# An earlier load of the second block's query features, four averages in one run, and the last keys' sums ahead of a turning, in a two-layer linear-attention and Mish kernel

## The chip, the core and the metric

The kernel runs on one core of a Trainium2 chip. The time is the device time of one execution in microseconds (us); the median of several runs counts. Before the change it is 1363.09 us (three runs, 1362.66 to 1363.34).

## What is computed

The input x has 2048 tokens (rows) of 640 numbers. Two layers are applied one after the other, each made of an attention part A and a dense part B, both with a layer norm ahead and a residual:

```python
x = x + A(layernorm(x)); x = x + B(layernorm(x))    # twice, same weights
# A: 32 heads of 20
pq = q @ w_phi;  pk = k @ w_phi                      # per head
phi_q = concat(softmax(pq), softmax(-pq));  phi_k = the same of pk      # 40 per head
kv = phi_k^T v  (summed over all tokens);  z = phi_k summed over all tokens
o = (phi_q kv) / (phi_q z + 1e-6);  out = o @ wo
# B: h = x w1 + b1;  act = h * tanh(softplus(h));  out = act @ w2       # 1536 hidden
```

No token's output o can be had before kv and z are complete, that is before the keys of the last token are summed.

## The kernel before

The 2048 tokens are 16 tiles of 128 (numbered 0 to 15), two tiles to a block (eight blocks, 0 to 7). In what follows K14 is the work on the keys of tile 14, Q14 on its queries, V14 on its values. TensorE is PE, VectorE DVE, ScalarE ACT, GpSimd POOL; all DMAs are issued from SyncE's queue, SP. A full-precision product is made of three matmuls of a high and a low part of each operand (line 399), and "splitting" is the making of these parts: a copy on ACT and a subtraction on another engine.

**First stage** (`attend_first`, line 448). For each block in turn the keys, values and queries of its two tiles are projected on PE (`project`, lines 387 to 400). `features` (lines 415 to 441) makes the softmax features out of a projection: ACT copies them out of PSUM, DVE takes maximum and minimum (429), POOL or DVE subtracts (430, 432), ACT takes the exponential, DVE sums and inverts (438, 439), POOL multiplies (440). Key features are then multiplied with the values and summed into one PSUM bank, `kva`, that stays open through the stage (line 475, 64 matmuls to a tile; two tiles follow one another directly). Query features are turned by a DVE transpose (484) and stored to DRAM with four DMAs (488), into `e_d[b]`.

These steps are Python generators. `advance` (461) resumes every pending generator once, the youngest first, after each new projection; so the yields say how far apart in the program the steps of one tile lie. The order of the last block is K14, K15, V14, V15, Q14 (line 649); Q15 is left to the second stage.

**Second stage** (`attend_second`, line 733). `finish_kv` (716) copies `kva`, turns it and masks it into `kvb`. `load(b)` (705) brings the turned query features of a block back: two tiles of five groups (712) and a small one (713). `average(b, t)` (743) multiplies them with `kvb` (753, 44 matmuls) into a PSUM tile of two banks and divides on DVE (762 to 767). `Transposed.step` turns the quotients of a block on PE (311) and splits them (127 on ACT, 317 on DVE). `Rows.half` (780) projects them with wo (399) and adds the residual. Between them the first stage's last projection Q15 is made and its features are finished bit by bit (`rest`, 687). In this order the stage starts: half of Q15, the sums of K14 and K15, `kva`'s copy, load(1), more of Q15, average(0,0), average(0,1), load(2), average(1,0), the turning of block 0, average(1,1), load(3), and then the loop over the blocks.

**Dense part** (`dense`, line 845), eight blocks of six pairs of hidden tiles. While the last pair runs, `load_v_weights` (185) loads and splits the value weights of the next layer (`split`, 134; `V_ORDER` is 0, 1, 4, 2, 3). Each of the five goes through a staging tile: two row tiles, two `v` tiles, one `big` tile.

**Buffers that the change touches.** `big` tiles (five): key features, every third tile's query features, loaded query features, the dense part's scratch. `x` tiles (two): the residual rows of a block. `r2` wide tiles 10 and 11: query features of the other tiles (`query_tile`, 412), later weights of the dense part. `v` tiles (two): value rows, and the turned inputs of the next block. PSUM: two `mm` tiles of two banks, four `one` tiles of one bank, of which `kva` holds one during the first stage.

**Order.** Everything lies in a block whose order is planned per engine on a simulated timeline when the kernel is built. In the second stage PE and SP keep the written order; DVE, ACT and POOL are planned everywhere in the lines that the change touches. An engine takes its instructions in that fixed order and waits where an operand isn't there.

Of the kernel before, what the change touches and what calls it, by code (L numbers as in the profile page):

```python
# [8 lines left out]
F32 = mybir.dt.float32  # L9
# [12 lines left out]
DH = 20  # L22
KD = D // P
KF = F // P
BT = 2
# [26 lines left out]
def kernel(  # L52
# [22 lines left out]
    def mm_tile():  # L75
        return psum.tile([P, 2, 512], F32, tag="mm", name="mm", bufs=2)
# [4 lines left out]
    def big_tile():  # L81
        return work.tile([P, EW], F32, tag="big", name="big", bufs=5)
# [4 lines left out]
    def pair_tile(dtype=F32R):  # L87
        return work.tile([P, 2, BLK], dtype, tag="ol", name="ol", bufs=6)
# [80 lines left out]
    def r2_wide(j, dtype=F32R):  # L169
        return wts.tile([P, 2, D], dtype, tag=f"r2{j}", name=f"r2{j}")  # L170
# [4 lines left out]
            return w[:, 0], w[:, 1]  # L175
        return tuple(wts.tile([P, D], F32R, tag=f"r2{s}{j}", name=f"r2{s}{j}") for s in "hl")

    def v_weights(ws, low=nc.vector):

        for k in V_ORDER:  # L180
            split(ws[k][0][:, D:2 * D], ws[k][1][:, D:2 * D], wv[k * P:(k + 1) * P, :],
                  (row_tile, row_tile, v_tile, v_tile, big_tile)[k], low)
            yield

    def load_v_weights():

        ws = [r1_pair(k) for k in range(KD)]
        for _ in v_weights(ws):
            pass
        return ws  # L190

# [218 lines left out]
        return g % 4, 2 * DH * (3 * (g // 4) + j)  # L410

    def query_tile(i):
        return big_tile() if i % 3 == 2 else r2_wide(10 + i % 3, F32).rearrange("p s d -> p (s d)")

    def features(ps, e, pool_sub):

# [31 lines left out]
    def attend_first(layer, x_src, first):  # L448
# [31 lines left out]
        def queries(xts, i, ps=None):  # L480
            e = query_tile(i)
            yield from features(project(xts, i % BT, q_ws, 0, w=FC) if ps is None else ps, e, True)

            nc.vector.transpose(e, e)  # L484
            b, t = divmod(i, BT)
            dst = e_d[b].rearrange("(j f) (t q s) -> t q f j s", f=32, t=BT, s=32)
            for q in range(4):
                nc.sync.dma_start(dst[t, q], e[32 * q:32 * q + 32].rearrange("f (j s) -> f j s", s=32))
                if b == NB - 1:
                    yield  # L490
# [150 lines left out]
        for b in range(0 if layer else 1, NB):  # L641
            xts = nxt
            order = ("k0", "k1", "v0", "v1", "q0", "q1")
            if b == 0:
                order = ("v0", "k0", "k1", "v1", "q0", "q1")
            elif b == 1 and layer == 0:
                order = ("k0", "q0", "k1", "v0", "q1", "v1")
            elif b == NB - 1:
                order = ("k0", "k1", "v0", "v1", "q0")
            vs = [v_tile() for _ in range(BT)]  # L650
            for n, (kind, t) in enumerate(order):
                t = int(t)
                i = b * BT + t
                if b == 0 and n == 1:
                    kva = one_tile()
                    nc.vector.memset(kva[:, :360], 0.0)
                if b == NB - 1 and n == 3:
                    loaded = {0: load(0)}
                if b + 1 < NB:
                    if n == 0 and b == 1 and layer == 0:  # L660
                        with tc.issue_after(ready):
                            xt = fetch_normed(b + 1)
                    elif n == 0:
                        xt = fetch_normed(b + 1)
# [37 lines left out]

        return kva, o_ws, loaded, rest()

    def load(b):

        ta, tb, tc_ = big_tile(), big_tile(), pair_tile(F32)
        for t, g0 in ((ta, 0), (tb, 5)):

            src = e_d[b][120 * g0:120 * (g0 + 4) + P]  # L710
            src = bass.AP(tensor=src.tensor, offset=src.offset, ap=[[BLK, P], [120 * BLK, 5], [1, BLK]])
            nc.sync.dma_start(t.rearrange("f (g s) -> f g s", s=BLK), src)
        nc.sync.dma_start(tc_[:80, 0], e_d[b][1200:])
        return [(ta, tb)[g // 5][:, (g % 5) * BLK:(g % 5 + 1) * BLK] for g in range(10)] + [tc_[:, 0]]
# [18 lines left out]
    def attend_second(x_src, x_dst, acc, fetches, makes, fetch_next, begin_next):  # L733
# [6 lines left out]
            with tc.issue_after(div[0]):  # L740
                next(rest, None)

        def average(b, t):

            phs = loaded[b]
            po = mm_tile()
            for g in range(G):
                n = 120 if g < 10 else 80
                w = GW if g < 10 else 42
                c, j = divmod(g, 8)  # L750
                for q in range(2):
                    s0 = t * P + 64 * q
                    nc.tensor.matmul(  # L753
                        po[64 * q:64 * q + 64, c, GW * j:GW * j + w], phs[g][:n, s0:s0 + 64],
                        kvb[:n, g, :w], start=True, stop=True)
            o = row_tile()
            den = work.tile([P, H], F32, tag="r", name="den", bufs=2)
            pv = [po[:, c, :(DH + 1) * n].rearrange("p (h d) -> p h d", d=DH + 1)
                  for c, n in ((0, 24), (1, 8))]
            hh = (slice(0, 24), slice(24, H))  # L760
            for c in range(2):
                nc.vector.tensor_scalar_add(den[:, hh[c]], pv[c][:, :, DH], DEN_EPS)
            nc.vector.reciprocal(den, den)
            for c in range(2):
                n = hh[c].stop - hh[c].start
                ins = nc.vector.tensor_tensor(o.rearrange("p (h d) -> p h d", d=DH)[:, hh[c]], pv[c][:, :, :DH],
                                        den[:, hh[c]].unsqueeze(2).to_broadcast([P, n, DH]), op=ALU.mult)
                div[0] = ins.ins
            rows.setdefault(b, []).append(o)
            if t == BT - 1:  # L770
                del loaded[b]

        class Rows:

# [16 lines left out]
        with tc.manual_schedule(engines={mybir.EngineType.PE, mybir.EngineType.SP}):  # L791
            kv = finish_kv(kva)
            next(rest)
            next(kv)
            loaded[1] = load(1)
            xs = {0: fetch(x_src, 0)}
            fetches[0]()
            next(rest)
            next(kv)
            next(rest)  # L800
            average(0, 0)
            average(0, 1)
            loaded[2] = load(2)
            average(1, 0)
            cur = Transposed(rows.pop(0)).all()
            average(1, 1)
            loaded[3] = load(3)
            for b in range(NB):
                if b == NB - 1:
                    ahead.all()  # L810
                elif b:
                    average(b + 1, 0)
                    average(b + 1, 1)
                r0, r1 = Rows(b, 0), Rows(b, 1)
                r0.half(0, one_tile())
                tail()
                if b + 1 < NB:
                    xs[b + 1] = fetch(x_src, b + 1)
                if 0 < b and b + 3 < NB:
                    loaded[b + 3] = load(b + 3)  # L820
                if b == NB - 3:
                    fetch_next()
                r0.half(1, one_tile())
                mv0 = r0.mean()
                if b == NB - 2:
# [12 lines left out]
                if b < NB - 1:  # L838
                    cur = nxt
            for _ in rest:  # L840
                pass
# [221 lines left out]
```

## Time and profile before

| what | value |
|---|---|
| median of 3 runs | 1363.09 us |
| profiled execution | 1363.75 us |
| its span in the trace | 1362.0 us |
| busy: PE, DVE, ACT, POOL | 1349.2, 1063.8, 584.5, 471.0 us |
| granted TensorE clock | 1.00 |

The span goes from the first to the last instruction of the trace; the profiled execution's own time is 1.75 us longer. The page gives the busy time of each engine and, in 40 slices, its share. The view of windows gives the same numbers for stretches that one chooses. The timeline lists an engine's instructions in order: start, duration, line, operation, output <- input, count, and in brackets for how long the engine was idle before and what ended that. Matmul ends are modelled, and matmuls overlap: one lasts 0.30 us and the next starts 0.14 us after it. The view of waits sums such idle times by what ended them; the chain of waits follows the end of the program back to what released each step.

In the trace the two layers lie one after the other. The first stage ends and the second begins at about 250 us in the first layer and at about 912 us in the second; between the layers lie about 683 to 701 us.

### The profile page before, as it was taken

How to read it: one execution, taken by the hardware profiler on the slowest of the kernel's cores; microseconds unless marked ns; L12 is line 12 of the kernel's file. 1: busy time of each engine (PE TensorE's matmuls, PEld its weight loads, DVE VectorE, ACT ScalarE, POOL GpSimd, SP SyncE). 2: the span in 40 equal slices, each digit the busy share in tenths (PEclk: the TensorE clock that was granted, in tenths of full speed). 3: DMA queues.
4: the chain of work that ended last, by engine and by line, in shares of the span. 5: the costliest groups of instructions: out<-in, count | busy, mean ns of one | idle time of the engine just before them, and what ended most of it. 6: DMA issues, size and time to landing. Idle time of an engine off the chain costs nothing.

```text
span 1362.0 us, 30917 instructions
## 1 busy us (share of the span) xinstructions
PE 1349.2 (99%) x12890; PEld 1337.6 (98%) x12890; DVE 1063.8 (78%) x1805; ACT 584.5 (43%) x1039; POOL 471.0 (35%) x361
## 2 busy tenths in 40 slices
PE   9999999999999999999999999999999999999998
PEld 8999999999999999999999999989999999999998
DVE  5988788877787887778778988878768776676775
ACT  5443444322454545445444344432236444444443
POOL 3345644434222222222216556744341211111111
PEclk9999999999999999999999999999999999999999
DMA  9614324798614542334472434459974231233200
GB/s 343 175 41 76 80 41 86 224 283 304 190 39 96 117 117 72 61 101 111 135 241 56 82 71 78 79 144 278 278 256 130 78 79 30 88 97 98 76 22 20
DMA packets 350613, 169.21 MB, mean 124 GB/s; under 512 B 287225, under 2 KB 323817, under 8 KB 350473
## 3 DMA queue, kind: packets, MB, share of 16 engines
q1 hardware_dynamic: 350473, 167.23, 45.8%
q8 instruction: 101, 1.65, 0.5%
q14 instruction: 39, 0.32, 0.1%
HBM read 104.61 MB, written 62.59 MB: 123 GB/s over the span
## 4 chain that ended last, share of the span: by engine, by line
PE 93%; DMA 2%; DVE 2%; POOL 1%; ACT 0%; issue 0%; SPq 0%; DVEq 0%; POOLq 0%; ACTq 0%
PE mm L399 26%; PE one L859 25%; PE mm L901 24%; PE one L399 12%; PE mm L753 3%; PE one L311 2%; PE one L475 2%; DMA big<-e_d 1%; DMA v<-in_wv 1%; DVE r L484 0%; DVE r L438 0%; DMA big<-in_phi_bd 0%; POOL r L440 0%; POOL big L440 0%; DVE m L429 0%
## 5 line engine op out<-in xcount | busy, mean ns | idle before, releaser
L901 PE MATMUL mm<-r2h,ol 128*128 128x320 f32 x1280 | 304.9, 309 | 0.0
L885 POOL TENSOR_TENSOR ol<-big,ol 128x512 fp32r<-128x512 f32 (+1 forms) x98 | 129.4, 1321 | 486.8 <-ACT ol L884 402.8
L859 PE MATMUL one<-xtl,r1h 128*128 128x256 f32 x960 | 268.2, 279 | 0.0
L859 PE MATMUL one<-xth,r1l 128*128 128x256 f32 x960 | 268.0, 279 | 0.0
L859 PE MATMUL one<-xth,r1h 128*128 128x256 f32 x960 | 265.9, 279 | 0.0
L901 PEld LDWEIGHTS mm<-r2h,ol 128*128 128x128 f32 x1280 | 219.2, 188 | 0.0
L901 PE MATMUL mm<-r2l,ol 128*128 128x320 f32 x640 | 197.3, 309 | 0.0
L399 PE MATMUL mm<-r1h,xth 128*128 128x304 f32 (+1 forms) x600 | 184.9, 308 | 0.0
L399 PE MATMUL mm<-r1l,xth 128*128 128x304 f32 (+1 forms) x600 | 183.7, 306 | 0.0
L399 PE MATMUL mm<-r1h,xtl 128*128 128x304 f32 (+1 forms) x600 | 183.5, 306 | 0.0
L859 PEld LDWEIGHTS one<-xtl,r1h 128*128 128x128 f32 x960 | 180.4, 188 | 0.0
L859 PEld LDWEIGHTS one<-xth,r1l 128*128 128x128 f32 x960 | 180.4, 188 | 0.0
L859 PEld LDWEIGHTS one<-xth,r1h 128*128 128x128 f32 x960 | 179.6, 188 | 0.0
L874 DVE TENSOR_SCALAR big<-big 128x512 f32<-128x512 f32 (+1 forms) x98 | 56.6, 578 | 111.5 <-ACT big L872 111.3
L440 POOL TENSOR_TENSOR big<-big,r 128x1280 f32<-128x1280 f32 x42 | 101.1, 2410 | 64.9 <-DVE r L439 38.9
L872 ACT ACTIVATE big<-one,b1s 128x256 f32<-128x256 f32 x192 | 80.9, 468 | 93.3 <-PE one L859 92.5
L901 PEld LDWEIGHTS mm<-r2l,ol 128*128 128x128 f32 x640 | 120.2, 188 | 0.0
L876 ACT ACTIVATE big<-big,two 128x512 f32<-128x512 f32 (+1 forms) x98 | 70.1, 716 | 115.7 <-DVE big L875 115.6
L884 ACT ACTIVATE ol<-big 128x512 fp32r<-128x512 f32 (+1 forms) x98 | 60.9, 622 | 133.4 <-DVE big L883 133.3
L399 PEld LDWEIGHTS mm<-r1h,xth 128*128 128x128 f32 x600 | 112.8, 188 | 0.6
L399 PEld LDWEIGHTS mm<-r1h,xtl 128*128 128x128 f32 x600 | 112.7, 188 | 0.3
L399 PEld LDWEIGHTS mm<-r1l,xth 128*128 128x128 f32 x600 | 112.8, 188 | 0.1
(154 smaller groups left out, 3118.5 us busy)
## 6 DMA issues: line engine op xcount, KB each, us to landing
big<-e_d SPq DMA_DIRECT2D x32, 640.0 KB, 7.7
x_d<-xt SPq DMA_DIRECT2D x23, 640.0 KB, 4.1
e_d<-r SPq DMA_DIRECT2D x88, 160.0 KB, 4.0
xt<-x_d SPq DMA_DIRECT2D x22, 640.0 KB, 5.4
n_d<-xn SPq DMA_DIRECT2D x176, 80.0 KB, 2.2
xt<-in_x SPq DMA_DIRECT2D x15, 640.0 KB, 4.2
xn<-x_d SPq DMA_DIRECT2D x28, 320.0 KB, 4.6
v<-n_d SPq DMA_DIRECT2D x30, 256.0 KB, 3.1
```

What stands on the lines that cost most here:

```text
L311: nc.tensor.transpose(ps[:, c, t * P:(t + 1) * P], self.rows[t][:, (c0 + c) * P:(c0 + c + 1) * P], ident)
L399: nc.tensor.matmul(ps[:, :w], a[:, sl], r, start=(k == 0 and n == 0), stop=(k == final and n == 2))
L440: nc.gpsimd.tensor_tensor(eg, eg, r.unsqueeze(2).to_broadcast([P, 2 * H, DH]), op=ALU.mult)
L475: nc.tensor.matmul(kva[32 * q:32 * q + DH + 1, c:c + 2 * DH], v[:, (DH + 1) * h:(DH + 1) * (h + 1)], e[:, 2 * DH * h:2 * DH * (h + 1)], st ...
L753: nc.tensor.matmul(po[64 * q:64 * q + 64, c, GW * j:GW * j + w], phs[g][:n, s0:s0 + 64], kvb[:n, g, :w], start=True, stop=True)
L859: nc.tensor.matmul(ph[:, j, :], l, r, start=(n == 0), stop=(n == 3 * KD - 1))
L872: exps[0] = nc.scalar.activation(part(ta, 0)[:, j - js.start], ph[:, j, :], AF.Exp, bias=b1s[:, 2 * pr + j:2 * pr + j + 1]).ins
L874: nc.vector.tensor_scalar_min(e, e, E_CAP)
L876: nc.scalar.activation(r, n, AF.Ln, bias=two)
L884: nc.scalar.activation(ah[:, js], n, AF.Copy)
L885: nc.gpsimd.tensor_tensor(al[:, js], n, ah[:, js].bitcast(F32), op=ALU.subtract)
L901: nc.tensor.matmul(pys[t][:, c, :HC], l[:, j, sl], r, start=(f == 0 and n == 0), stop=(f == KF - 1 and n == 2))
```

## The change

Five things change. (1) `load_v_weights` stages two of the value weights in the halves of one `x` tile instead of two `v` tiles. (2) The query features of tiles 12 to 15 use only the two wide tiles: Q14 goes from `big` to wide tile 10, Q15 from 10 to 11. (3) Q13 yields once more ahead of its turning. (4) load(1) is issued in the last block of the first stage, ahead of Q14, with an `x` tile for its first half. (5) The four averages of blocks 0 and 1 follow one another; the third takes two `one` banks instead of an `mm` tile; the divide becomes a function of its own, and that of average(1,1) is written behind the turning of block 0. load(2) is still written behind average(0,1), load(3) now ahead of the turning.

```diff
     def load_v_weights():
         ws = [r1_pair(k) for k in range(KD)]
-        for _ in v_weights(ws):
+        xt = x_tile()
+        for _ in v_weights(ws, stages=(row_tile, row_tile, lambda: xt[:, 0], lambda: xt[:, 1], big_tile)):
             pass
...
     def query_tile(i):
-        return big_tile() if i % 3 == 2 else r2_wide(10 + i % 3, F32).rearrange("p s d -> p (s d)")
+        if i < NT - 4 and i % 3 == 2:
+            return big_tile()
+        return r2_wide(10 + (i % 3 if i < NT - 4 else i % 2), F32).rearrange("p s d -> p (s d)")
...
             yield from features(project(xts, i % BT, q_ws, 0, w=FC) if ps is None else ps, e, True)
+            if i == NT - 3:
+                yield
...
                     loaded = {0: load(0)}
+                if b == NB - 1 and n == 4:
+                    loaded[1] = load(1, lambda: x_tile().rearrange("p t d -> p (t d)"))
...
-    def load(b):
-        ta, tb, tc_ = big_tile(), big_tile(), pair_tile(F32)
+    def load(b, first=big_tile):
+        ta, tb, tc_ = first(), big_tile(), pair_tile(F32)
...
-        def average(b, t):
+        def average(b, t, alone=False):
             phs = loaded[b]
-            po = mm_tile()
+            po = [one_tile(), one_tile()] if alone else (lambda mm: [mm[:, 0], mm[:, 1]])(mm_tile())
...
+            if t == BT - 1:
+                del loaded[b]
+            return lambda: divide(b, po)
+
+        def divide(b, po):
             o = row_tile()
...
             next(kv)
-            loaded[1] = load(1)
             xs = {0: fetch(x_src, 0)}
...
-            average(0, 0)
-            average(0, 1)
+            average(0, 0)()
+            average(0, 1)()
             loaded[2] = load(2)
-            average(1, 0)
+            average(1, 0, True)()
+            second = average(1, 1)
+            loaded[3] = load(3)
             cur = Transposed(rows.pop(0)).all()
-            average(1, 1)
-            loaded[3] = load(3)
+            second()
```

More of the change, by code (lines that the diff above doesn't have):

```diff
@@ L176, in r2_pair, with v_weights @@
         return tuple(wts.tile([P, D], F32R, tag=f"r2{s}{j}", name=f"r2{s}{j}") for s in "hl")
-    def v_weights(ws, low=nc.vector):
+    def v_weights(ws, low=nc.vector, stages=None):
+        if stages is None:
+            stages = (row_tile, row_tile, v_tile, v_tile, big_tile)
         for k in V_ORDER:
             split(ws[k][0][:, D:2 * D], ws[k][1][:, D:2 * D], wv[k * P:(k + 1) * P, :],
-                  (row_tile, row_tile, v_tile, v_tile, big_tile)[k], low)
+                  stages[k], low)
             yield
@@ L753, in average @@
                     nc.tensor.matmul(
-                        po[64 * q:64 * q + 64, c, GW * j:GW * j + w], phs[g][:n, s0:s0 + 64],
+                        po[c][64 * q:64 * q + 64, GW * j:GW * j + w], phs[g][:n, s0:s0 + 64],
                         kvb[:n, g, :w], start=True, stop=True)
+            if t == BT - 1:
+                del loaded[b]
+            return lambda: divide(b, po)
+        def divide(b, po):
             o = row_tile()
             den = work.tile([P, H], F32, tag="r", name="den", bufs=2)
-            pv = [po[:, c, :(DH + 1) * n].rearrange("p (h d) -> p h d", d=DH + 1)
+            pv = [po[c][:, :(DH + 1) * n].rearrange("p (h d) -> p h d", d=DH + 1)
                   for c, n in ((0, 24), (1, 8))]
@@ L769, in average @@
             rows.setdefault(b, []).append(o)
-            if t == BT - 1:
-                del loaded[b]
         class Rows:
@@ L811, in attend_second @@
                 elif b:
-                    average(b + 1, 0)
-                    average(b + 1, 1)
+                    average(b + 1, 0)()
+                    average(b + 1, 1)()
                 r0, r1 = Rows(b, 0), Rows(b, 1)
```

## The prediction, on record before the run

> **What bounds the kernel now.** I read the page first, for the engine that is never free.
>
> ```profile
> span 1362.0 us, 30917 instructions
> PE 1349.2 (99%) x12890; PEld 1337.6 (98%) x12890; DVE 1063.8 (78%) x1805; ACT 584.5 (43%) x1039; POOL 471.0 (35%) x361
> ```
>
> PE idles for 1362.0 - 1349.2 = 12.8 us of the whole span. The change neither adds nor removes a matmul, so nothing but this idle time can be won. The view of windows says where it lies (span of the stretch, then PE busy; 1.00 is the granted clock):
>
> ```profile
> 226.00:263.00 37.00, 35.68 (x621) 34.63 (x611) 30.03 (x53) 12.81 (x22) 13.43 (x8) 1.00 0.67 178
> ...
> 889.00:925.00 36.00, 32.77 (x545) 31.72 (x532) 28.73 (x51) 11.51 (x20) 12.17 (x6) 1.00 0.67 174
> ```
>
> At the change from the first to the second stage PE idles 37.00 - 35.68 = 1.32 us in the first layer and 36.00 - 32.77 = 3.23 us in the second. These are two of the three places that the change touches; the third, between the layers, comes below with 0.51 us. All three hold 5.06 us, the ceiling of any gain from waits. The timeline of PE at the second layer's change of stages splits the 3.23:
>
> ```profile
> 908.19 0.30 PE L399 MATMUL one<-r2h,xtl 128*128 128x304 f32 x1
> 909.88 1.48 PE L475 MATMUL one<-big,v 128*21 128x40 f32 x128 [1.39 <-POOL big L440]
> ...
> 913.90 1.39 PE L753 MATMUL mm<-kvb,big 120*64 120x63 f32 x40
> ...
> 915.21 1.36 PE L753 MATMUL mm<-kvb,big 120*64 120x63 f32 x40
> ...
> 917.10 0.80 PE L753 MATMUL mm<-kvb,big 120*64 120x63 f32 x20 [0.43 <-PE mm L753]
> 919.31 0.80 PE L753 MATMUL mm<-kvb,big 120*64 120x63 f32 x20 [1.40 <-DMA big<-e_d]
> ...
> 920.14 1.31 PE L311 MATMUL one<-ident,xn 128*128 128x128 f32 x10
> 921.38 1.39 PE L753 MATMUL mm<-kvb,big 120*64 120x63 f32 x40
> ...
> 922.79 0.41 PE L399 MATMUL one<-r2h,xth 128*128 128x320 f32 x1
> ...
> 923.19 0.31 PE L399 MATMUL one<-r2h,xtl 128*128 128x320 f32 x1
> ```
>
> Three waits are to be seen: 1.39 us for POOL's multiply of K15, 0.43 us of the third average for an `mm` tile (two of them, the first still being divided), 1.40 us for the second half of load(1). The same three in the first layer:
>
> ```profile
> 246.50 0.30 PE L399 MATMUL one<-r2h,xtl 128*128 128x304 f32 x1
> 247.48 1.48 PE L475 MATMUL one<-big,v 128*21 128x40 f32 x128 [0.68 <-POOL big L440]
> 254.71 0.80 PE L753 MATMUL mm<-kvb,big 120*64 120x63 f32 x20 [0.43 <-PE mm L753]
> 255.72 0.80 PE L753 MATMUL mm<-kvb,big 120*64 120x63 f32 x20 [0.21 <-DMA big<-e_d]
> ```
>
> **The change part by part.**
>
> *K15's sums ahead of Q13's turning.* DVE and POOL in the second layer:
>
> ```profile
> 900.91 1.27 ACT L127 ACTIVATE big<-big 128x1280 f32<-128x1280 f32 x1 [1.10 <-DVE big L432]
> 902.66 0.55 DVE L439 RECIPROCAL r<-r 128x64 f32<-128x64 f32 x1
> 903.83 1.51 DVE L484 STREAM_TRANSPOSE r<-r 128x1280 f32<-128x1280 f32 x1 [0.62 <-POOL r L440]
> 905.26 1.44 DVE L438 TENSOR_REDUCE r<-big 128x64 f32<-128x1280 f32 x1
> 901.42 2.37 POOL L440 TENSOR_TENSOR r<-r,r 128x1280 f32<-128x1280 f32 x1 [4.81 <-DVE r L439]
> 903.75 2.37 POOL L440 TENSOR_TENSOR big<-big,r 128x1280 f32<-128x1280 f32 x1
> 907.47 2.36 POOL L440 TENSOR_TENSOR big<-big,r 128x1280 f32<-128x1280 f32 x1 [1.35 <-DVE r L439]
> ```
>
> POOL multiplies Q13, K14, K15, and idles 1.35 us before K15: DVE waited 0.62 us for Q13's product and turned it (1.51) before it took K15's sum (905.26), although the exponential of K15 was there at 900.91 + 1.27 = 902.18. With one more yield Q13's turning is written behind K15's sum, in the same `advance` where K15, the younger, comes first. DVE then goes on at 902.66 + 0.55 = 903.21: sum until 904.65, reciprocal until 905.20. POOL is free of K14 at 903.75 + 2.37 = 906.12, so POOL itself is late next; K15 starts there and PE at about 908.5, 1.35 us earlier, where PE has just come from 908.19 + 0.30. In the first layer POOL starts its three at 239.01:
>
> ```profile
> 239.01 2.38 POOL L440 TENSOR_TENSOR r<-r,r 128x1280 f32<-128x1280 f32 x1 [5.10 <-DVE r L439]
> ```
>
> Three back to back end at 239.01 + 3 x 2.37 = 246.1, before PE comes at 246.80: the 0.68 goes whole. Values -1.35 and -0.68; the other end is 0, if the planned order of DVE stays; a loss could only come through the stores that are late (rival 4). Q13's turning and its four stores come about 1.4 us later; what waits for them is below, with Q15's tile.
>
> *load(1) in the last block.* Its data have been in DRAM for long (block 1 of eight). First tile: an `x` tile, free, since the last rows of the first stage are read before its last block, and in the second layer it takes no `x` tile at all. Second tile: the `big` tile that Q14 no longer takes; counted round the five it is K13's, summed before K15 is projected. So it lands some 15 us before the averages. Both waits go: -1.40 and -0.21, the other end 0. Its three issues leave the queue where the residual rows, a weight and load(2) then move up.
>
> ```profile
> 900.14 8.56 SPq L488 DMA_DIRECT2D e_d<-r  x8
> 910.79 1.87 SPq L712 DMA_DIRECT2D big<-e_d  x2
> big<-e_d SPq DMA_DIRECT2D x32, 640.0 KB, 7.7
> ```
>
> The page's row gives a median of 7.7 us to landing, which from the second issue, over by 910.79 + 1.87 = 912.66, reaches 919 to 920; the wait ends at 919.31. The Trainium skill, page "DMA: Bandwidth & Descriptors", section "Bandwidth", lists 0.95 us for 64 KB and 6.15 us for 1 MB; between them 640 KB would take about 4.1 us, an estimate from that page. By it the second tile would have been there at about 916.8, before the third average asks for it at 917.7, and the load's part of the sum would be 0 instead of -1.61. The measured landing decides.
>
> *Third average in single banks, four in one run.* Two `one` banks are free by then (`kva` copied, its turned form read), so -0.43 in each layer; other end 0. The fourth takes an `mm` tile after the first's divide: DVE starts one divide every 1.48 us, and the first is done before the third average ends.
>
> ```profile
> 915.44 0.26 DVE L762 TENSOR_SCALAR den<-mm 128x24 f32<-128x24 f32 x2 [1.04 <-PE mm L753]
> 916.92 0.24 DVE L762 TENSOR_SCALAR den<-mm 128x24 f32<-128x24 f32 x2
> 920.83 1.36 ACT L127 ACTIVATE xth<-one 128x512 fp32r<-128x512 f32 x3 [5.25 <-PE one L311]
> L127 ACT ACTIVATE xth<-one 128x512 fp32r<-128x512 f32 x2 | 1.1, 594 | 5.3 <-PE one L311 5.3
> 921.81 0.68 DVE L317 TENSOR_TENSOR xtl<-one,xth 128x512 fp32r<-128x512 f32 x1
> ```
>
> But this takes a cover away, and adds a wait. Before, average(1,1) lay between the turning of block 0 and the projection that reads its split (921.38 to 922.79); now the projection follows the turning at once, and everything of PE is queued behind it. From the turning's start: PE is ready after 1.24 us (920.14 to 921.38). ACT begins the first copy after 0.69 (920.83) and takes 0.594, so the high part is there at 1.28; DVE adds 0.68, so the low part is there at about 2.0. The third matmul wants it at 1.24 + 0.40 (922.79 to 923.19) = 1.64. The new wait is some 0.4 to 0.5 us in all; I take **+0.45** in each layer. Ends: 0, and +1.3 if DVE puts the fourth divide ahead of the subtraction (fourth divide done 1.54 + 4 x 1.48 = 7.46 after the first average's start, turning begun at 4 x 1.31 = 5.24 [913.90 to 915.21 is one average], low part at 2.2 + 0.68 = 2.9 instead of 2.0, and its start-up).
>
> *Value weights in an x tile.*
>
> ```profile
> 695.78 0.74 ACT L138 ACTIVATE r1h<-v 128x640 fp32r<-128x640 f32 x1 [2.54 <-DMA v<-in_wv]
> 696.57 0.71 PE L399 MATMUL one<-r1h,xth 128*128 128x320 f32 x3 [0.51 <-ACT r1h L138]
> ```
>
> The load of two of the weights goes into `v` tiles, which the turned inputs of the next block hold until they are split; the `x` tile of block 6 has long been stored. ACT idles 2.54 us ahead of its copy, PE 0.51 behind it: with the data there, -0.51. Ends 0 and -0.51, or +0.74, one ACT copy put ahead of the last Mish.
>
> *Q14 and Q15 in wide tiles 10 and 11.* A query tile is written once the stores of the tile that lay there before are read.
>
> ```profile
> e_d<-r SPq DMA_DIRECT2D x88, 160.0 KB, 4.0
> 906.43 0.68 ACT L127 ACTIVATE big<-mm 128x608 f32<-128x608 f32 x1 [3.35 <-PE mm L399]
> ...
> 913.53 1.27 ACT L127 ACTIVATE big<-big 128x1280 f32<-128x1280 f32 x1 [5.67 <-DVE big L432]
> 914.71 0.72 ACT L127 ACTIVATE r<-one 128x304 f32<-128x304 f32 x2
> ```
>
> They now wait until Q12's and Q13's stores are read (ACT's copy of Q14 was at 906.43, its exponential at 913.53, the copies of Q15 at 914.71). Q12's four stores come out from 900.14 as before, are issued by 903.5 and land by about 907.5: Q14's copy waits about 1 us, and only average(0,1), 9 us later, wants its `mm` tile. Q13's turning ends at about 906.7; four issues (before, the last four of the eight ran from the turning's end at 903.83 + 1.51 = 905.34 to 900.14 + 8.56 = 908.70) end at about 910.1, and the last lands some 4 us later, 914.1. Q15's copy would be ready at 914.71 - 1.35 = 913.4 and so waits about 0.7 us on ACT. Queued behind it on ACT are the splits of the turning, wanted at about 918.5 (first average 913.90 - 1.35 = 912.55, turning 5.24 later, ACT 0.69 after that): cost 0, with 918.5 - 914.1 - 0.72 = 3.7 us of cover.
>
> **The sum.** Second layer: -1.35 - 0.43 - 1.40 + 0.45 = -2.73. First: -0.68 - 0.43 - 0.21 + 0.45 = -0.87. Weights: -0.51. Together **-4.1 us**: span 1362.0 to 1357.9, the profiled execution 1363.75 to 1359.65. That execution lies 0.66 us above the median 1363.09, so on the median 1359.0.
>
> **The rivals.**
> 1. *The fourth divide goes first* on DVE: +0.85 more in each layer (1.3 for 0.45), sum -2.4, 1360.7. For it: DVE is free some 0.6 us before the first subtraction can start. Against: in the text it stands behind it.
> 2. *DVE's order stays*, because it is planned and not written: -1.35 and -0.68 are lost, sum -2.1, 1361.0. The change then doesn't do what its last words say.
> 3. *The load was not the late one*: its tiles arrive and PE waits all the same, sum -2.5, 1360.6. The bracket of 919.31 speaks against it. The Trainium skill's page "DMA: Bandwidth & Descriptors" would have it so.
> 4. *Slower: the stores of Q12 and Q13 are held on SP.* SP takes issues in order. If the second tile of load(1) gets a buffer that comes free only with the sums of K14 and K15 (as load(1) did at 910.79), and stands in the queue ahead of these eight stores, Q12's are issued only from about 910.4 to 913.8 and land at 917.8. ACT then copies Q14 at 917.8 instead of 906.43; Q14's exponential, ahead of Q15's copies on ACT, came 7.1 us after that copy, some of it queueing, so I put it at 5 to 7 us: 923 to 925, and the splits of the turning behind it (1.27 + 0.72) at 925 to 927 instead of 918.5. With the shorter delay, 6.5 us in each layer, the sum is -4.1 + 13 = +8.9: 1372. Break-even is a delay of 2 us per layer past the cover. Against: one `big` tile more is free than before.
>
> **Chances.** Forecast 0.60, divide first 0.12, order stays 0.08, load not late 0.03, held stores 0.17. What a measurement of this kernel can tell from no change is about 0.2%, 2.7 us. The forecast lies beyond it, rivals 1 to 3 within it: faster 0.60, same 0.23, slower 0.17. The range: below, no new wait at all (-5.0, 1358.1) and the spread of runs (0.3), 1357.8; above, rival 2 with the ACT copy's 0.74, 1361.8. It leaves out the held stores.
>
> **What would show it.** Right: no bracket before the sums of K14 and K15 beyond 0.1 us, four averages without a bracket, about 0.4 us at the first projections after the turning; POOL's three multiplies back to back; PE idle 0.5 us in each change of stages and 0 between the layers. Wrong: a DVE turning still ahead of the sum; ACT waiting for a DMA before Q14's or Q15's copy; a gap of over 1 us ahead of the projection.

## The result: slower by 12 us, and the profile after

| | before | after |
|---|---|---|
| median | 1363.09 us (1362.51 to 1364.45, 5 runs) | 1375.35 us (1373.8 to 1376.15, 5 runs) |
| profiled execution | 1363.75 us | 1375.35 us |
| its span | 1362.0 us | 1373.2 us |
| granted TensorE clock, mean | 1.00 | 0.996 |

The ratio is 1.0088, with a 95% interval of 1.0076 to 1.0099. The forecast was 1359.0 and its range ended at 1361.8: it is wrong in sign and in size. First the two lines of the page that answer to those of before:

```profile
span 1373.2 us, 30942 instructions
...
PE 1352.4 (98%) x12890; PEld 1339.7 (98%) x12890; DVE 1064.8 (78%) x1805; ACT 584.4 (43%) x1039; POOL 471.8 (34%) x361
```

The number of matmuls is the same and their busy time has grown by 3.2 us, so some of them ran slower; PE's idle time went from 12.8 to 1373.2 - 1352.4 = 20.8 us. The view of waits of the changed kernel names the idle time (us in total, times, longest):

```profile
PE one L402 <- DVE xtl L320: 7.0, 2, 3.7
PE mm L762 <- issue: 2.3, 1, 2.3
PE one L480 <- POOL big L445: 1.8, 2, 1.3
...
PE one L732 <- DVE xn L728: 1.1, 1, 1.1
```

Two lines of before are gone: the waits on block 1's load (1.6 us in two) and those of the third average for its bank (0.9 in two). Three are new: 7.0 us of the first projections for the split, 2.3 us that nothing ends, and 1.1 us for the copy of `kva`. The wait for POOL's multiply of K15 has only gone from 2.1 to 1.8. The windows show the first layer's change of stages and the time behind the second layer's (granted clock third from the end of a line; in the kernel before, both stretches are at 1.00), then the first layer in slices of 2 us:

```profile
226.00:263.00 37.00, 32.71 (x557) 31.54 (x545) 30.79 (x54) 12.39 (x22) 13.84 (x7) 0.96 0.71 187
...
925.00:1011.00 86.00, 81.24 (x999) 79.19 (x999) 64.65 (x163) 20.54 (x33) 32.78 (x29) 0.98 0.77 241
```

```profile
258.00:260.00 2.00, 0.39 (x2) 0.13 (x2) 2.00 (x5) 0.54 (x2) 0.55 (x1) 1.00 1.08 357
260.00:262.00 2.00, 0.00 (x0) 0.00 (x0) 2.00 (x4) 0.00 (x0) 0.72 (x1) 0.58 0.37 136
262.00:264.00 2.00, 1.91 (x7) 1.91 (x8) 2.00 (x5) 0.00 (x0) 0.00 (x0) 0.50 0.05 20
264.00:266.00 2.00, 2.00 (x10) 2.00 (x9) 0.19 (x2) 0.00 (x0) 1.70 (x1) 0.50 0.03 8
266.00:268.00 2.00, 2.00 (x12) 2.00 (x12) 1.97 (x3) 0.00 (x0) 0.66 (x1) 0.71 0.00 0
268.00:270.00 2.00, 2.00 (x16) 2.00 (x15) 1.55 (x4) 0.00 (x0) 0.00 (x0) 1.00 0.00 0
```

PE does nothing from 258.4 to 262.1, and then gets half its clock until about 267: 7 and 10 matmuls in a slice of 2 us where 16 fit at 1.00. In the kernel before PE was busy for all of 258 to 266, at 1.00. What PE waited for is told by the timelines of PE and of DVE at that place:

```profile
256.49 1.31 PE L314 MATMUL one<-ident,xn 128*128 128x128 f32 x10
...
258.08 0.31 PE L402 MATMUL one<-r2l,xth 128*128 128x320 f32 x1
262.09 0.64 PE L402 MATMUL one<-r2h,xtl 128*128 128x320 f32 x1 [3.70 <-DVE xtl L320]
262.52 0.47 PE L402 MATMUL one<-r2h,xth 128*128 128x320 f32 x1
```

```profile
257.71 0.89 DVE L781 TENSOR_TENSOR xn<-mm,den 128x480 f32<-128x480 f32 x2
258.51 1.53 DVE L434 TENSOR_REDUCE m<-r 128x32 f32<-128x640 f32 x2
259.96 1.48 DVE L443 TENSOR_REDUCE r<-r 128x64 f32<-128x1280 f32 x1
261.36 1.61 DVE L320 TENSOR_TENSOR xtl<-one,xth 128x512 fp32r<-128x512 f32 x3
```

DVE is never idle here. It takes the fourth divide (from 257.04 on), then the maximum and minimum of Q15 (1.53 us), then the sum of Q14 (1.48), and only then the subtraction of the split, 3.6 us after the end of the turning. The second layer has the same row of four at 927.88, 929.36, 930.81 and 932.20, and a wait of 3.26. The timeline of DVE in the kernel before has the split first, as soon as there was something to subtract, and the same two groups behind the fourth divide:

```profile
258.22 1.61 DVE L317 TENSOR_TENSOR xtl<-one,xth 128x512 fp32r<-128x512 f32 x3
...
260.42 0.89 DVE L766 TENSOR_TENSOR xn<-mm,den 128x480 f32<-128x480 f32 x2
261.23 1.54 DVE L429 TENSOR_REDUCE m<-r 128x32 f32<-128x640 f32 x2
262.68 1.48 DVE L438 TENSOR_REDUCE r<-big 128x64 f32<-128x1280 f32 x1
```

The reason is in the text: `tail` ties the pending features to `div[0]`, the last divide. Before, the last divide was written behind the turning and planned behind the split; now it is planned ahead of it, and the features that are tied to it may follow at once. Lines 434 and 443 of the changed kernel are lines 429 and 438 of the kernel before, and line 320 is line 317.

The account of the 11.2 us of span, from four rows:

```profile
246.91 1.48 PE L480 MATMUL one<-big,v 128*21 128x40 f32 x128 [0.54 <-POOL big L445]
...
914.63 1.48 PE L480 MATMUL one<-big,v 128*21 128x40 f32 x128 [1.26 <-POOL big L445]
918.67 0.54 PE L732 MATMUL one<-ident,xn 128*120 128x128 f32 x3 [1.10 <-DVE xn L728]
...
926.47 0.63 PE L762 MATMUL mm<-kvb,xt 120*64 120x63 f32 x15 [2.30 <-issue]
```

- Up to the last keys' sums of the first layer: 247.48 to 246.91, -0.57; of this -0.14 is the wait for POOL, the rest is a shorter start of the program, which the change doesn't touch.
- From there to the same sums of the second layer: -0.57 to 914.63 - 909.88 = +4.75, that is +5.32. The third average's and the load's waits of the first layer are gone (-0.64); +3.70 for the split; some 18 matmuls at half clock, about 0.12 us more each, make +2.3; the value weights (-0.51, and a new wait of +0.34) and POOL's wait in the second layer (-0.13) take 0.3 off; the last 0.3 is in no row that I can name.
- From there to the end of the span: +4.75 to +11.2, that is +6.45: -1.83 for the same two waits, +1.10 for `kva`'s copy, +2.30 of the stall, +3.26 for the split, and 1.6 for the clock, which was at 0.50 again from 933 to 935.

The copy of `kva` is late because a subtraction of Q14 now stands ahead of it on DVE, and that waited 3.57 us for POOL; before, the copy came first. This, too, is a planned order that changed.

### The profile page after: what moved, and what is told of

Its sections match the earlier page's. It is cut to its first block, busy times and chain, and to the rows that moved or that the text cites. A ratio compares the mean times of both kernels' runs of the same rounds, so it can differ in the third digit from the quotient of the medians.

```text
span 1373.2 us, 30942 instructions
## 1 busy us (share of the span) xinstructions
PE 1352.4 (98%) x12890; PEld 1339.7 (98%) x12890; DVE 1064.8 (78%) x1805; ACT 584.4 (43%) x1039; POOL 471.8 (34%) x361
## 5 line engine op out<-in xcount | busy, mean ns | idle before, releaser
L402 PE MATMUL one<-r2h,xtl 128*128 128x320 f32 (+1 forms) x350 | 110.0, 314 | 7.0 <-DVE xtl L320 7.0
L445 POOL TENSOR_TENSOR big<-big,r 128x1280 f32<-128x1280 f32 x40 | 96.3, 2410 | 59.2 <-DVE r L444 33.4
L402 PE MATMUL one<-r2h,xth 128*128 128x320 f32 (+1 forms) x350 | 113.0, 323 | 1.1 <-DVE r2l L276 1.0
```

What stands on the lines that cost most here:

```text
L402: nc.tensor.matmul(ps[:, :w], a[:, sl], r, start=(k == 0 and n == 0), stop=(k == final and n == 2))
L445: nc.gpsimd.tensor_tensor(eg, eg, r.unsqueeze(2).to_broadcast([P, 2 * H, DH]), op=ALU.mult)
```

## The experiments

My theory from these views: the loss is DVE's planned order (what stands ahead of the split), made longer by the clock that halves behind the wait; the gains of the load and of the banks are real, the gain of K15's sums isn't there. The main rival was that four averages in one run cost by themselves, by whatever reason (buffers, banks, traffic). Three batches were run, each with the kernel before on the same chip: 1363.3 us in the first two (18 and 33 runs), 1362.98 in the third (27 runs). Each batch was on another chip, and the changed kernel was not run again in them; the kernel before differs by 0.3 us between them.

### The fourth divide tied behind the split

```diff
-            self.low.tensor_tensor(lo, ps[:, :n], hi.bitcast(F32), op=ALU.subtract)
+            self.last = self.low.tensor_tensor(lo, ps[:, :n], hi.bitcast(F32), op=ALU.subtract).ins
...
-            second()
+            with tc.issue_after(cur.last):
+                second()
```

> The changed kernel with one edge more: the fourth divide is queued on DVE behind the last subtraction of the split of block 0 (and with it the pending feature work of Q14 and Q15, which is tied to that divide). No other line differs. Theory (DVE's planned order): the third matmul of the first projection waited 3.70 and 3.26 us because the fourth divide, Q15's maximum and minimum and Q14's sum stood ahead of the split on DVE, and the granted clock fell to 0.50 behind that wait, which cost another 2.4 and 1.5 us. With the split first the waits fall to about 0.45 each and the clock stays at 1.00: 1375.35 - 5.65 - 4.3 = about 1365.4; the 2.30 us without a releaser in the fourth average of the second layer and the 1.10 us for kva's copy stay. Rival (early loads or wide tiles are to blame, the order only follows): waits and clock as in the changed kernel, 1374 to 1376.

Measured: 1367.07 us (8 runs), 1.0027 of before (1.0016 to 1.0037). The wait of the first layer, in the timeline of PE:

```profile
258.97 0.42 PE L402 MATMUL one<-r2h,xtl 128*128 128x320 f32 x1 [0.17 <-DVE xtl L320]
```

8.3 us of the 12 come back by one edge in DVE's order, with all five parts of the change in place. The theory holds for the larger part. What is left in the second layer is the wait for POOL (1.26), that for `kva`'s copy (1.11), and a stall:

```profile
921.24 0.90 PE L762 MATMUL mm<-kvb,xt 120*64 120x63 f32 x16 [2.19 <-issue]
```

Behind this stall the clock was at 0.51 from 923 to 925, which did not follow the changed kernel's stall of 2.30 us; that slow stretch is part of the 1.7 us by which the run lies above the expectation.

### Only the features tied behind the split

Here the fourth divide stays ahead of the split, as in the changed kernel; Q15's maximum and minimum and Q14's sum go behind it (`cur.last` is set as above).

```diff
             second()
+            div[0] = cur.last
```

> The changed kernel, with the last block features tied to the split of the turning: on VectorE only the fourth divide stays ahead of the split, the max and min of query tile 15 and the sum of query tile 14 go behind it. Theory: the wait of the first projection falls by the 2.85 us that these two groups took (261.36 less 258.51), to 0.8 us in the first layer and 0.4 in the second, no wait is long enough to halve the clock there, and the time is within 1 us of the kernel with the whole divide behind the split (1367.1): 1366.5 to 1368.5. Rival: the divide by itself is enough to cost a long wait and the clock, 1371 or more.

Measured: 1365.69 us (11 runs), 1.0014 (1.0005 to 1.0023), a little below the expectation. In the first layer the wait is 1.06 us and the clock stays:

```profile
258.85 0.41 PE L402 MATMUL one<-r2h,xtl 128*128 128x320 f32 x1 [1.06 <-DVE xtl L320]
```

```profile
260.00:262.00 2.00, 2.00 (x15) 2.00 (x15) 2.00 (x3) 0.00 (x0) 1.27 (x1) 1.00 0.29 106
```

So the divide that my first rival named costs 1.1 us where it is to be seen, inside the bounds that I gave it (0 to 1.3); in the second layer, where a stall of 2.10 us comes first, there is no wait for the split at all. The other 9.7 us went when the two groups of features went behind the split. Not all of it is theirs: this kernel's trace is also without the 1.10 us for `kva`'s copy, since DVE's plan has that copy first again. No case of mine had the two groups there.

### The fourth average back behind the turning

```diff
-            second = average(1, 1)
-            loaded[3] = load(3)
             cur = Transposed(rows.pop(0)).all()
-            second()
+            average(1, 1)()
+            loaded[3] = load(3)
```

> The changed kernel with the fourth average and load(3) put back behind the turning of block 0, where they were before; the other parts stay. Theory (the cover was lost): the fourth average lies again beside the split, so no wait at the first projection at all and clock 1.00: about 1 us below the kernel with only the divide moved, 1364 to 1365, less 1.1 if kva's copy comes ahead of Q14's subtraction as listed, so 1363 to 1364. Rival (early loads or wide tiles): no better than 1374.

Measured: 1363.65 us (11 runs), 1.0007 (0.9999 to 1.0016). As expected: without the run of four the loss is gone, and what is left of the change (the other four parts, and the third average's own banks) gains nothing that can be told. In the trace, of a run 2.1 us above this median, a stall of 1.91 us and a slow stretch behind it stand in the second layer.

### The run of four alone, on the kernel before

> The kernel before with part 5 alone: four averages in one run, the third in single banks, the fourth's divide written behind the turning; load(1), the query tiles, the yield and the value weights as before. Theory (the run alone is the cause): DVE's order has again the fourth divide, Q15's maximum and minimum and a sum ahead of the split; waits of 3 to 4 us and the clock at 0.50 behind them in both layers, about 5.5 us each: 1363.1 + 11 - 0.9 (third average's wait) = about 1373. Rival (it takes the early load and the wide tiles): 1362 to 1364.

Measured: 1377.11 us (4 runs), 1.0103 (1.0089 to 1.0116), some 2 us slower than the whole change, though the two intervals overlap. The waits of the first projections, the clock behind the first of them, and the load's waits are all there:

```profile
PE one L399 <- DVE xtl L317: 6.7, 2, 3.4
...
PE one L753 <- DMA big<-e_d: 1.9, 2, 1.0
```

```profile
262.00:264.00 2.00, 0.38 (x2) 0.38 (x3) 2.00 (x3) 0.00 (x0) 0.26 (x1) 0.99 1.11 321
264.00:266.00 2.00, 2.00 (x10) 2.00 (x9) 1.70 (x4) 0.00 (x0) 0.16 (x1) 0.50 1.12 353
```

This part alone makes the loss; that the other four take some 2 us off it these few runs don't establish. The direction is the theory's, the size is 4 us above it; 1.12 us for `kva`'s copy, a stall of 0.86 us and 1.0 us for a weight load at the start of the program are in this trace and were not in the expectation.

### The wait filled with matmuls

The changed kernel with 24 turnings of the identity, whose result nobody reads, between the turning of block 0 and the first projection of each layer.

> The changed kernel with 24 extra transposes of the identity on PE between the turning of block 0 and the first projection in both layers; what they write is overwritten by the projection. They take about 24 x 0.125 = 3.0 us and lie in the wait of 3.70 and 3.26 us; DVE's order stays as in the changed kernel. Theory (the clock falls because PE idles that long): the clock stays at 1.00 and only the wait is left, 2.4 + 1.5 us less: about 1371.4. Rival (the clock falls for another reason, or the time is all wait): clock 0.50 as before, 1375 or later.

Measured: 1368.84 us (4 runs), 1.0043 (1.0029 to 1.0057). More work, and 6.5 us less time. The slices of the same place are at full clock:

```profile
260.00:262.00 2.00, 0.46 (x4) 0.20 (x2) 2.00 (x4) 0.00 (x0) 0.69 (x1) 1.00 0.43 163
262.00:264.00 2.00, 1.95 (x13) 1.95 (x14) 2.00 (x4) 0.00 (x0) 0.00 (x0) 1.00 0.02 10
264.00:266.00 2.00, 2.00 (x16) 2.00 (x15) 1.11 (x3) 0.00 (x0) 1.73 (x1) 1.00 0.00 0
```

With the waits cut to 1.59 us each the clock isn't lowered, so the slower matmuls came from the wait and not from what followed it. Part of the 6.5 us is another matter: in this kernel the stall (0.3 instead of 2.3) and `kva`'s wait (1.1) were absent too, and the wait for POOL fell from 1.8 to 1.2.

### The yield alone, on the kernel before

> The kernel before with the third part alone: query tile 13 is turned one step later, everything else as in the kernel before. Theory (from the trace of the changed kernel): VectorE's planned order puts that turning between the last keys' sum and its reciprocal, and the sum waits 0.61 us for a buffer that GpSimd frees, so TensorE's wait for the last keys' multiply shrinks by some 0.14 us a layer only: 1362.8 to 1363.2, that is no change that can be told. Rival (the term on record): 1.35 us in the second layer and 0.68 in the first, 1361.0 to 1361.3.

Measured: 1364.88 us (11 runs), 1.0017 (1.0008 to 1.0025). No gain, as expected, and somewhat more loss than expected: the waits on the load have grown from 1.6 to 3.0 us. It is not issued later against PE's work (911.40, with the last keys' sums at 910.50; before, 910.79 and 909.88), but Q13's stores are issued until 910.89 instead of 908.70 and lie closer ahead of it; that they slow it is not shown. DVE shows why the sums gain so little:

```profile
904.57 1.49 DVE L438 TENSOR_REDUCE r<-big 128x64 f32<-128x1280 f32 x1 [0.61 <-POOL r L440]
905.98 1.50 DVE L486 STREAM_TRANSPOSE r<-r 128x1280 f32<-128x1280 f32 x1
907.40 0.51 DVE L439 RECIPROCAL r<-r 128x64 f32<-128x64 f32 x1
```

K15's sum does stand ahead of Q13's turning now. But it waits 0.61 us for one of the two `r` tiles, which POOL frees at the end of Q13's multiply, and the planner has put the turning between the sum and its reciprocal, which is what POOL waits for.

### The turning tied behind the reciprocal

The kernel with the fourth average behind the turning, and one edge more:

```diff
-        nc.vector.reciprocal(r, r)
+        last_rec[0] = nc.vector.reciprocal(r, r).ins
...
             if i == NT - 3:
                 yield
-            nc.vector.transpose(e, e)
+                with tc.issue_after(last_rec[0]):
+                    nc.vector.transpose(e, e)
+            else:
+                nc.vector.transpose(e, e)
```

> The changed kernel with the fourth average and its load back behind the turning, and query tile 13's turning tied on VectorE behind the last keys' reciprocal. Theory: the reciprocal comes 1.5 us earlier, in time for GpSimd's multiply to follow the one before without a gap, so TensorE's waits for it (0.56 and 1.27 us in the same kernel without the tie) fall below 0.2: 1.6 us less than that kernel's 1363.65, that is 1361.6 to 1362.4. Rival (GpSimd's own row of multiplies, 2.37 us each, sets the end, or the later turning makes something else late): 1363.3 to 1364.

Measured: 1361.15 us (11 runs), 0.9985 (0.9977 to 0.9994), and so 2.5 us less than without the tie (in another batch, beside the same 1363.3 of before). The timeline of POOL:

```profile
900.03 2.37 POOL L446 TENSOR_TENSOR r<-r,r 128x1280 f32<-128x1280 f32 x1 [4.81 <-DVE r L445]
902.36 4.70 POOL L446 TENSOR_TENSOR big<-big,r 128x1280 f32<-128x1280 f32 x2
```

Q13, K14 and K15 are multiplied back to back, which the forecast had promised of the yield, and no wait for POOL is left in PE's list. The wait for the `r` tile (0.61) is still there and costs nothing, since POOL isn't free earlier. The 2.5 us are more than the tie was to bring (1.6): the stall of 1.91 us isn't in this trace either, and which part of the gain is POOL's and which is the stall's the medians can't tell.

### The loads later

> The changed kernel with the fourth average behind the turning, the load of block 2 issued behind the fourth average and that of block 3 inside the loop of block 0. Theory: the stall of 1.91 us that no instruction or transfer ends (in the turning of the second layer, while the load of block 2 keeps the DMA engines full) is a fetch of TensorE's own instructions that stands behind that load's packets; without the load there it goes, and with it the dip of the clock to 0.56 behind it: 3 us less than 1363.65, some 1360.0 to 1361.5. Rival (the stall has nothing to do with the traffic): it stays, 1363.3 to 1364. A third way: the later loads are late themselves, and waits on them of 1 us or more appear at the averages of blocks 2 and 3.

Measured: 1364.73 us (11 runs), 1.0010 (1.0001 to 1.0019). The stall is there, in the timeline of PE:

```profile
920.83 0.38 PE L314 MATMUL one<-ident,xn 128*128 128x128 f32 x2 [1.81 <-issue]
```

But the run didn't do what it was for. The load of block 2 is written behind the fourth average, and SP doesn't wait for PE there: it came to that load right behind Q13's stores, at 911.48, where the kernel with the fourth average behind the turning has it at 911.95. Only the load of block 3 came later, at 922.81 instead of 916.08. The timeline of SP:

```profile
907.09 4.28 SPq L495 DMA_DIRECT2D e_d<-r  x4
911.48 2.22 SPq L721 DMA_DIRECT2D big<-e_d  x2
...
922.81 1.55 SPq L721 DMA_DIRECT2D big<-e_d  x2
```

So the load of block 3 is not what makes the stall, which ends at 920.83 while the DMA engines are idle (a share of 0.00 from 920 to 922). My theory, that the load of block 2 delays a fetch, was not tested.

### The early load alone

> The changed kernel's early load of block 1 and its value weights and query tiles alone; turnings, averages and their order are those of the kernel before. Theory: the waits on block 1's transfer (1.38 and 0.2 us) are gone, but in the second layer the stall that nothing ends (1.8 to 2.3 us) comes in their place, so that the sum is nearly nil: 1362.5 to 1364.5, with the 0.43 us waits of the third average for its bank still there. Rival (the terms on record hold by themselves): no such stall, 1361.3 to 1361.9.

Measured: 1363.99 us (11 runs), 1.0007 (0.9998 to 1.0016). Waits on block 1's transfer are gone in both layers; so the load was the late one, and my third rival falls as it was worded. By its price it does not fall in the second layer, where a stall that comes 30 matmuls further on takes 1.29 of the 1.4 us back:

```profile
PE one L480 <- POOL big L445: 2.1, 2, 1.4
...
PE one L314 <- issue: 1.3, 1, 1.3
```

### Both ties, and the fourth average inside the turning

> The changed kernel, run of four averages kept, with two ties on VectorE: the fourth divide (and with it the last block features) behind the split of the turning, and query tile 13's turning behind the last keys' reciprocal. Theory: both causes of loss are gone, POOL's wait (1.26 us) and with it the place at which the stall of 2.19 us fell, so it comes to the kernel with the reciprocal tie alone (1361.15): 1360.5 to 1362. Rival (a run of four costs by itself, whatever VectorE's order): as the kernel with the split tied alone, less 1.6: 1365.5.

Measured: 1361.38 us (11 runs), 0.9992 (0.9983 to 1.0001): the run of four with DVE's order mended in both places is as good as the kernel without it (1361.15, in another batch), and the rival that the run costs by itself is out. A stall of 1.49 us remains in the second layer.

Then, with the same two ties, the fourth average between the second and third step of the turning:

```diff
-            second = average(1, 1)
-            loaded[3] = load(3)
-            cur = Transposed(rows.pop(0)).all()
+            cur = Transposed(rows.pop(0))
+            cur.step()
+            cur.step()
+            second = average(1, 1)
+            cur.step()
+            loaded[3] = load(3)
```

> As the kernel with both ties, but the fourth average stands between the second and the third step of the turning, ahead of the step that waited 0.65 us in each layer for the third divide (in the kernel with the reciprocal tie alone). Theory: those waits go under the average's matmuls (2 us): 1.3 us less than 1361.15, some 1359.5 to 1360.3, and the last part of the split is still in time, as the projection comes to it 1.7 us after its start. Rival (the third part of the split is late, since the turning ends 2 us later): a wait of 0.5 to 1.5 us in the projection of each layer takes their place, 1361 to 1363.

Measured: 1361.03 us (11 runs), 0.9984 (0.9975 to 0.9993). The windows show that the two changes of stages are nearly without idle time, 0.09 and 0.44 us instead of 1.32 and 3.23:

```profile
226.00:263.00 37.00, 36.91 (x590) 35.98 (x578) 31.27 (x55) 12.60 (x22) 13.85 (x7) 1.00 0.73 187
889.00:925.00 36.00, 35.56 (x503) 34.48 (x502) 31.05 (x54) 11.25 (x19) 13.41 (x7) 1.00 0.74 192
```

This and the kernel with the reciprocal's tie alone are the best versions found; between the two no difference can be told, and of the further 1.3 us that I expected of it next to nothing came (two waits of 0.3 us for the residual add, behind the stretches shown, and 0.34 of the stall are new). Both beat the kernel before by about 0.15%, 2 us.

## Why the prediction was wrong, step by step

- **The cover that was lost** is the step that failed: "+0.45 in each layer", with "+1.3 if DVE puts the fourth divide ahead" as its upper end. It measured 3.70 and 3.26 us of wait, and 2.3 and 1.6 us of halved clock behind it. With the split first, the wait was 0.17 us in the first layer and none in the second (there at a lowered clock), so the +0.45 itself was not too small; the order that it took for granted was not the one that came. The bound was too near because I priced a plain swap of two neighbours on DVE. The fourth divide is an anchor: `tail` ties the pending features to the last divide, so when the divide moved ahead of the split, the features moved with it. The code that says so was in reach, and the price stood in DVE's rows of the kernel before, 1.54 us and 1.48 us.
- **The first rival** ("the fourth divide goes first") named the right place and the wrong amount. "Against: in the text it stands behind it" was no argument, since DVE's order is planned and not written; I used that fact in the second rival and not in the first.
- **What followed a wait of over 3 us** was in no part of the sum: I took the clock as 1.00 throughout, since all rows of before show it so.
- **K15's sums**: -1.35 and -0.68, measured -0.13 and -0.14. The second rival ("DVE's order stays, because it is planned") was the case in effect, though the text's order did change: the reciprocal was passed by the turning. The mechanism itself was right: with the reciprocal tied, POOL multiplies back to back and PE waits no more for it.
- **The load**: -1.40 and -0.21. Both waits went. But in the second layer a stall of 1.3 to 2.3 us came in all six kernels that load early and have neither the reciprocal's tie nor the filling, so that nothing was left of it there in their traces. A shorter stall, 0.86 us, stood in the run of four alone, which does not load early, so the early load is not needed for one.
- **The third average's bank**: -0.43 in each layer, right.
- **The value weights**: -0.51. The wait is gone (PE is busy 17.99 of the 18 us from 683 to 701, before 17.49), but 5 us later PE waits 0.34 us for DVE's residual add (at 705.84), where it had not waited before: 0.17 is left. Even that is not safe. ACT still waits for the last of the weights, now in the `big` tile (2.02 us), and four other kernels with the same staging have PE's wait for it again (0.37 us with the early load alone, 0.49 with the loads later, 0.26 and 0.19 in two more), with the new wait of 0.33 us besides.
- **The held stores** (rival 4, the only slower case): did not occur. The stores of Q12 and Q13 were issued from 905.02 and 911.68, each right behind its turning. My chance of slower was right to be there and hung on the wrong mechanism.
- **The signs**: "a DVE turning still ahead of the sum" wasn't seen in that form, "a gap of over 1 us ahead of the projection" was.

## What to carry to other kernels

Where an engine's order is planned, look up what each moved instruction carries with it: ties to "the last divide" or "the last sum" move everything that hangs on them, and a gain or a loss is bounded by all that may pass, not by the one instruction that the diff names. Moving a step ahead of a consumer paid here only when the short instruction on the critical path was tied in front of the long ones that nobody waited for: two such edges turned a loss of 12 us into 1.6 us below the kernel before, just short of what the runs can tell, and with the fourth average inside the turning into a gain of 2 us. Filling a wait with matmuls does not end it sooner, but it can save the slow matmuls behind it, here 2.3 and 1.6 us.

## What the runs showed of the hardware that was not expected

**The clock halves behind a wait.** After waits of 3.70 and 3.26 us matmuls started every 0.27 us instead of 0.147, for 5.0 and 3.1 us, with a granted clock of 0.50. Waits of 1.4 us (before) and 1.59 us (filled) left it at 1.00. The Trainium skill, page "TensorE: Matmul & The Clock Gate", section "HAM oscillation — how this bites in real kernels", gives the rule that no idle gap of PE should exceed about 3.4 us. The traces agree with it in kind: the gaps of 3.70 us here and of 3.44 us in the run of four alone lowered the clock. Shorter gaps did it too: 3.26 us, 2.19 us (the fourth divide behind the split), 2.10 us (only the features behind it) and 1.91 us (the fourth average behind the turning). But a gap of 2.30 us in the changed kernel did not, nor did one of 1.81 us in the kernel with the later loads, in nearly the same place as that of 1.91. So the length of the gap alone does not decide in these runs; what else does stays open. The windows behind the gap of 1.91 us, behind that of 1.81, and behind that of 2.30:

```profile
920.00:922.00 2.00, 1.20 (x10) 0.87 (x11) 0.66 (x2) 0.54 (x2) 0.00 (x0) 0.81 1.10 348
922.00:924.00 2.00, 2.00 (x42) 2.00 (x42) 1.02 (x2) 0.33 (x2) 0.00 (x0) 0.50 0.73 222
```

```profile
920.00:922.00 2.00, 1.17 (x20) 1.00 (x21) 0.79 (x2) 0.53 (x2) 0.00 (x0) 1.00 0.00 1
922.00:924.00 2.00, 2.00 (x45) 1.95 (x41) 1.83 (x6) 0.34 (x2) 0.00 (x0) 1.00 0.43 54
```

```profile
925.00:927.00 2.00, 0.53 (x19) 0.53 (x20) 0.99 (x3) 0.00 (x0) 0.00 (x0) 1.00 1.04 355
927.00:929.00 2.00, 2.00 (x39) 1.79 (x35) 1.05 (x4) 0.54 (x2) 0.00 (x0) 1.00 0.95 273
```

**A stall that nothing ends.** In seven kernels PE stood for 1.3 to 2.3 us in the second layer's averages or turning, with "issue" as the only reason. The DMA view, asked in steps of 0.25 us, shows one packet of an instruction queue (q8) some 2.5 to 2.8 us ahead of the end of the stall in six of them (918.25 for 920.80, 918.0 for 920.83, 923.75 for 926.47), and 3.5 us in the seventh; the 0.86 us in the run of four alone end 2.6 us behind one too. Where the packet came earlier against PE's work (912.25 with the reciprocal's tie, 914.5 with the 24 added matmuls), the stall was 0 or 0.3 us. In the six the packet came 5.7 to 7.0 us after the issue of the load of block 2, in those two 1.9 and 0.3 us after it. This speaks for PE running out of fetched instructions there, with a fetch that came behind that load's packets. It is argued and not shown: no run took that load away, and what makes the packet late stays open.
